# Moving GpSimd's eleven sums of x in an fp32 convolution + GELU kernel from the second product to the first

## The chip, the cores and the metric

The kernel runs on one core of one Trainium2 chip. The metric is device time in microseconds (us) of that core, the median over several executions. Four engines do the work and run independently of each other, each through its own instructions in program order: TensorE (PE in the profile) multiplies matrices, VectorE (DVE) and ScalarE (ACT) do elementwise work and read TensorE's results from PSUM, GpSimd (POOL) does elementwise work in SBUF and issues transfers of its own. SyncE (SP) only issues transfers. An engine that meets an instruction whose inputs are not there waits, and all that stands behind it on that engine waits too.

## The reference

A causal convolution of length 7 along the sequence, with one softmaxed filter for each of 8 groups of 24 channels, and behind it a two-layer block with a sigmoid-GELU, all in fp32:

```python
w = softmax(weight, axis=-1)                       # (8, 7)
x_pad = zeros(6) ++ x                              # x: (8, 4096, 192)
conv[b, s, h, :] = sum_k w[h, k] * x_pad[b, s + k, h, :]
h = conv.reshape(32768, 192) @ w_in                # (192, 2048)
g = h / (1 + exp(-1.702 * h))
out = g @ w_out                                    # (2048, 192)
```

## The kernel before

**Tiling.** The 32,768 tokens are worked through in 32 steps (`big` = 0 to 31) of 1,024 tokens. A step has two products. The *first product* makes h from the convolved x; the *second product* makes the output from g. Both are computed by bilinear schemes that save multiplications: in place of the plain block products, sums of blocks of one factor are multiplied with sums of blocks of the other, and the results are added up.

**First product.** x of a step is six blocks of 128x256 (two for each third of the 192 channels), numbered 0 to 5, and eleven sums of them, numbered 6 to 16. `SUMS_C` (line 148) lists the sums as (target, a, sign, b); block 6 is block 0 minus block 4, block 7 is block 6 minus block 5, and so on. `next_sum` (line 553) emits one, on GpSimd in all steps behind the first two. The twenty `TERMS` (line 179) pair a piece of w_in with a block of x. The product has two halves, v = 0 and v = 1, and each uses all twenty terms. `FIRST` (line 643) writes the order out by hand: "prod" is a term on TensorE (`product1`, line 588), "sum" an addition on VectorE that joins a PSUM tile and a tile in SBUF (line 636), "copy" a copy on ScalarE (line 630), "gelu" the activation that writes g (lines 612 and 617). Entries marked 1 belong to the next half and are done ahead, so the second half's terms on blocks 0, 3, 6, 7, 8, 9 and 10 run inside the first half, and seven terms of the next step open its first product. `FILL` (line 660) hangs other work in at positions of this list; `hidden` (line 757) walks both.

The six own blocks of two consecutive steps have separate places, but the eleven sums of consecutive steps share one place: the sums for step n+1 may overwrite those of step n once step n's last term on the block is through.

Each block is needed at both partition halves. `cross` (line 520) sends a group of neighbouring blocks to the other half by two transfers on SyncE's queue. Seven groups wait in a list (`pieces`): three of plain blocks, put there by `cross_blocks` (line 543), and four of sums, put there by `next_sum` when the last sum of a group is emitted. `cross_piece` (line 539) sends the list's next group.

**Second product.** g is sixteen blocks of 128x1024 (`spot(5)` to `spot(20)`); `spot(0)` to `spot(4)` are scratch of the same size. `PLAN` (line 944) is the second product's order, written out by hand. ("sum", d, a, sign, b) is an addition of two such blocks on VectorE (lines 361 and 363); ("acc", d, a) adds block a into d by a transfer that GpSimd issues (line 986); ("main", form, spot, ...) and ("side", ...) choose what TensorE multiplies next, and each ("go", n) runs n groups of four products (`go`, line 1026). "seed" is a ScalarE copy (line 1039), "join" a VectorE addition of results, "turn" a VectorE transpose, "store" the output transfer on SyncE. Between them stands work for later steps: "tap" is one of the convolution's 21 multiplications on ScalarE (line 487), "tree" adds taps by a transfer from GpSimd (line 509), "vsum" calls `next_sum`, "cross" calls `cross_piece`. After the list the loop from line 1063 does what is left of both.

**Early sums of g.** Six operations on g that need only early blocks are listed in `EARLY_G` (line 942) and hung into the first product's second half, as ("g", i): five VectorE sums and one transfer from GpSimd (block 0 into block 8).

**GpSimd's order in a step.** Twelve additions of taps (line 504) in the first product; the transfer into block 8; then in the second product the eleven sums of x mixed with six transfers of g and with the tree.

**The loop** (line 1285) emits, for each step, both halves of the first product, then puts the plain blocks of step n+1 and after them its sums on their lists, then emits the second product.

Of the kernel before, what the change touches and what calls it, by code (L numbers as in the profile page):

```python
# [15 lines left out]
def kernel(  # L16
# [49 lines left out]
    def load_x(big, ns=range(2)):  # L66


        p, c = divmod(big, CHUNKS)
        if c == 0 and 0 in ns:  # L70
            (nc.gpsimd if big else vec).memset(xin[0:R, :, 0, :], 0.0)
        for n in ns:
            for o in range(2):
                j = 1 if c == 0 and o == 0 else 0
                t = c * TOK + o * T + (j - 1) * Q
                for v in range(2):
                    q0 = o * R + v * Q
                    nc.sync.dma_start(
                        out=xin[q0 : q0 + Q, n, j:NJ, :],
                        in_=x_v[n, p, t : t + (NJ - j) * Q, v * Q : v * Q + XW].rearrange(  # L80
                            "(j i) d -> i j d", i=Q
                        ),
                    )
# [13 lines left out]
    g = consts.tile([P, NG, 2, 2, NG, T], F32)  # L97
# [341 lines left out]
    def transpose_x(big, c, n=None):  # L439
        if big not in xts:  # L440
            xts[big] = xt_pool.tile([P, NC, 2, XT], F32, name="xt")
        ns = slice(0, 2) if n is None else slice(n, n + 1)
        vec.transpose(
            xts[big][:, c, ns, :].rearrange("p n (j t) -> p (n j) t", t=Q),
            xin[:, ns, :, :].rearrange("p n j d -> p (n j) d")[:, :, c * R : c * R + Q],
        )
# [54 lines left out]
    def next_add():  # L501
        if adds:
            dst, home = adds.pop(0)
            nc.gpsimd.tensor_add(dst, dst, home)  # L504
# [10 lines left out]
    def sums_c(big, dst, a, op, b):  # L515
        add_up(
            lambda j: conv_t[:, slot_of(big, j), :], dst, a, op, b, eng=vec if big == 1 else nc.gpsimd,
        )

    def cross(big, b0, b1):  # L520
        s0, x0 = slot_of(big, b0), cross_of(big, b0)
        for o in range(2):
            nc.sync.dma_start(
                out=conv_t[halves[1 - o], x0 : x0 + b1 - b0, :], in_=conv_t[halves[o], s0 : s0 + b1 - b0, :]
            )
# [13 lines left out]
    def cross_piece():  # L539
        if pieces:  # L540
            cross(*pieces.pop(0))

    def cross_blocks(big):

        bs = list(REST)
        while bs:
            n = 1
            while n < min(3, len(bs)) and bs[n] == bs[0] + n:
                n += 1
            pieces.append((big, bs[0], bs[0] + n))  # L550
            bs = bs[n:]

    def next_sum():
        if sums_left:
            big, i = sums_left.pop(0)
            sums_c(big, *SUMS_C[i])
            for b in GROUPS:
                if max(LAST_AT[s] for s in b) == i:
                    pieces.append((big, b[0], b[-1] + 1))

    def begin_sums(big):
        sums_left.extend((big, i) for i in range(len(SUMS_C)))
# [75 lines left out]
    def plain(u, m, n, v, slot, ks=range(NC), first=0):  # L638

        for k in ks:  # L640
# [21 lines left out]
            1: (("add", 4), ("add", 4), ("add", 4)), 9: (("turn", 0),), 15: (("turn", 1),), 21: (("turn", 2),),  # L662
        },
        {
            3: (("g", 0),), 12: (("g", 1),), 17: (("g", 2),), 18: (("g", 3),), 31: (("g", 4),), 36: (("g", 5),),
        },
    ]
    FILL_1 = [
# [3 lines left out]
            32: (("work", 0.8),), 35: (("tap",),), 36: (("tap",),), 40: (("tap",),), 42: (("work", 0.8),),  # L672
        },
        {
            3: (("g", 0),), 13: (("g", 1),), 16: (("g", 2),), 17: (("g", 3),), 22: (("g", 4),), 23: (("g", 5),),
            29: (("turn", 0),), 31: (("turn", 1),), 35: (("turn", 2),),
        },
    ]

# [6 lines left out]
    def begin_half():  # L686
        return {}, dict(COUNT)
# [35 lines left out]
    def seeds_ahead(big, half):  # L723

        while later and later[0][0] == "copy":
            dst = later[0][1]
            if dst[0] == "a" and dst not in half[0] and not free:
                return
            do(big, 0, half, *later.pop(0))

    def rest_ahead(big, half):
        while later:
            do(big, 0, half, *later.pop(0))
# [6 lines left out]
    def fill(big, kind, *args):  # L740
        if kind == "work":
            work(*args)
        elif kind == "tap":
            next_tap()
        elif kind == "add":
            for _ in range(*args):
                next_add()
        elif kind == "turn":
            need(f"done {big + 1}")
            if big + 2 < N_BIG:  # L750
                transpose_x(big + 2, *args)
                if args[0] == NC - 1 and big + 3 < N_BIG:
                    load_x(big + 3)
        else:
            sum_g(*(EARLY_G if big > 1 else EARLY_G_1)[args[0]])

    def hidden(big, v, now, nxt):

        for i, (ahead, *item) in enumerate(FIRST):
            for what in (FILL if big > 1 else FILL_1)[v].get(i, ()):  # L760
                fill(big, *what)
            if not ahead:
                do(big, v, now, *item)
            elif v == 0:
                do(big, 1, nxt, *item)
            elif nxt and ahead == 2:
                do(big + 1, 0, nxt, *item)
            elif nxt:
                later.append(item)
# [162 lines left out]
    def store(big, n, o=None, queues=(nc.sync,) * 3):  # L932
# [6 lines left out]
        for c in range(NC):  # L939
            queues[c].dma_start(out=rows[c], in_=osb[c * Q : (c + 1) * Q, n, js, :])  # L940

    EARLY_G = [(6, 6, "-", 10), (1, 7, "-", 6), (1, 1, "-", 11), (0, 5, "+", 6), (8, 0, "acc"), (2, 9, "-", 0)]
    EARLY_G_1 = EARLY_G[:4] + [(8, 8, "+", 0)] + EARLY_G[5:]
    PLAN = [
        ("side", 13, 16, "k0"), ("main", 1, 5, "p2", 1), ("vsum",), ("cross",), ("go", 3), ("vsum",), ("go", 1),
# [37 lines left out]
    def sum_g(dst, a, op, b=None):  # L983

        if op == "acc":
            nc.gpsimd.dma_start(out=spot(dst), in_=spot(a), accum_op=ALU.add)  # L986
        else:
            add_up(spot, dst, a, op, b)
# [84 lines left out]
    def work(us):  # L1073
        while todo and todo[0][1] <= us + 0.2:
            us -= todo[0][1]
            todo.pop(0)[2]()

    def next_tap():
        if ready:
            ready.pop(0)[2]()  # L1080
            while ready and ready[0][1] == 0:
                ready.pop(0)[2]()

    def need(label):
        for q in (todo, ready):
            while any(item[0] == label for item in q):
                q.pop(0)[2]()
# [177 lines left out]
    def begin(big):  # L1265
        todo.extend(prepare(big))
        ready.extend(prepare_taps(big))
# [17 lines left out]
    for big in range(1, N_BIG):  # L1285
        more = big + 1 < N_BIG
        rest_ahead(big, half)
        other = begin_half()
        hidden(big, 0, half, other)
        half = begin_half() if more else None  # L1290
        hidden(big, 1, other, half)
        if more:
            need(f"done {big + 1}")
            cross_blocks(big + 1)
            begin_sums(big + 1)
        need("forms")
        if big + 2 < N_BIG:
            begin(big + 2)
        bx, bs, by = (free.pop(0) for _ in range(3))

        def final():
            free.append(bs)
            if more:
                seeds_ahead(big + 1, half)

        second(big, bx, bs, by, final, not more)
        free += [bx, by]
# [30 lines left out]
```

## Time and profile before

| what | us |
|---|---|
| median of 3 executions | 2384.64 (2384.21 to 2385.5) |
| the profiled execution, its own time | 2383.57 |
| its span, first to last instruction | 2381.9 |
| start of the first product in steps 2 and 31 | 189.1 and 2307.3 |
| first product of one step (992.99 to 1028.69) | 35.70 |
| second product of the same step (1028.69 to 1065.8) | 37.1 |
| second product of the last step (2342.80 to 2376.80) | 34.0 |
| granted TensorE clock, mean | 0.996 |

Steps 2 to 30 are 29 periods with the same work; the mean is (2307.3 - 189.1) / 29 = 73.04 us. In 22 of them the second product takes 37.1 us, in seven 37.8 to 38.3; the first product takes 35.7 to 35.9 in all.

Times in the views are counted from the first instruction. In a list of groups a line holds line of code, engine, operation, output and inputs, shapes, count, then busy us and mean ns of one, then idle time in front of them and what ended it. In a timeline a line holds start and length in us, engine, line, operation, count, and in brackets the engine's idle time before it and what released it. In a table of windows the columns are the window, its length, and for each engine its busy us with its instructions.

### The profile page before, as it was taken

The numbers are of one execution on the slowest core, as the hardware profiler recorded it, in microseconds if no ns is written. First come the engines' busy times: TensorE is split into PE (matmuls) and PEld (weight loads), VectorE is DVE, ScalarE is ACT, GpSimd is POOL, SyncE is SP. The second block draws the span as 40 slices with busy tenths as digits, with TensorE's granted clock in tenths as the row PEclk, the third lists the DMA queues.
The fourth block names the chain that finished last, engine by engine and source line by source line (L and its number), as shares of the span: only waits on it lengthen the run. The fifth ranks groups of instructions, "written<-read, shape, count | busy, mean of one in ns | idle before, by whom it ended". The sixth has DMA issues, their size and how long they took to land.

```text
span 2381.9 us, 62150 instructions
## 1 busy us (share of the span) xinstructions
PE 2285.4 (96%) x24966; PEld 1353.0 (57%) x24966; DVE 2049.1 (86%) x2842; ACT 1779.4 (75%) x3481; POOL 1133.5 (48%) x1101
## 2 busy tenths in 40 slices
PE   9899999999999999999999999999999999999999
PEld 4355555555555555555555555555555555555555
DVE  8798889988889888889888898888988889988888
ACT  8478777778777787777787777877777777778755
POOL 1454554444554446645445544556344454444520
PEclk9899999999999999999999999999999999999999
DMA  8875667655666556675556665566755567654543
GB/s 197 149 151 118 119 131 148 123 118 112 136 127 136 117 117 121 127 148 119 119 117 134 133 128 121 111 129 128 145 115 118 115 131 149 123 118 88 112 101 68
DMA packets 281073, 298.84 MB, mean 125 GB/s; under 512 B 120145, under 2 KB 212305, under 8 KB 280785
## 3 DMA queue, kind: packets, MB, share of 16 engines
q0 software_dynamic: 58080, 151.48, 35.2%
q1 hardware_dynamic: 221056, 143.00, 26.3%
q8 instruction: 197, 3.23, 0.5%
q14 instruction: 92, 0.75, 0.1%
q10 hardware_dynamic: 1648, 0.39, 0.1%
HBM read 53.15 MB, written 25.17 MB: 33 GB/s over the span
## 4 chain that ended last, share of the span: by engine, by line
PE 49%; DVE 35%; issue 7%; ACT 5%; DMA 4%; SPq 1%; POOL 0%; DVEq 0%; ACTq 0%; POOLq 0%
PE slot L595 37%; DVE g L363 16%; PE slot L1010 11%; DVE g L361 7%; DVE room L363 3%; DVE room L361 2%; DVE osbs L361 2%; ACT g L612 2%; DVE slot L636 2%; DVE room L636 1%; ACT g L617 1%; DMA conv_t<-conv_t 1%; DMA g<-osbs 1%; ACT slot L630 1%; DMA g<-g 1%
## 5 line engine op out<-in xcount | busy, mean ns | idle before, releaser
L595 PE MATMUL slot<-conv_t,w_in_s 64*128 64x512 f32 x5152 | 1154.4, 597 | 4.6 <-ACT room L630 2.3
L595 PEld LDWEIGHTS slot<-conv_t,w_in_s 64*128 64x128 f32 x5152 | 699.6, 186 | 448.4 <-issue 221.5
L1010 PE MATMUL slot<-g,w_form 128*32 128x256 f32 x9672 | 920.4, 380 | 11.4 <-DVE room L363 10.5
L1010 PEld LDWEIGHTS slot<-g,w_form 128*32 128x32 f32 x9672 | 474.1, 110 | 186.4 <-DVE room L363 25.0
L1010 PE MATMUL slot<-g,w_out_s 128*32 128x256 f32 x5952 | 470.8, 381 | 62.8 <-DVE g L363 57.6
L363 DVE TENSOR_TENSOR g<-g 128x1024 f32<-128x1024 f32 x372 | 514.2, 1408 | 8.5 <-DMA g<-osbs 3.3
L636 DVE TENSOR_TENSOR slot<-slot,room 128x512 f32<-128x512 f32 x496 | 321.9, 694 | 220.5 <-ACT g L612 118.8
L612 ACT ACTIVATE g<-slot 128x512 f32<-128x512 f32 x776 | 429.3, 610 | 75.3 <-PE slot L595 75.1
L1035 ACT COPY room<-slot 32x256 f32<-32x256 f32 x651 | 236.9, 364 | 324.8 <-PE slot L1010 233.2
L504 POOL TENSOR_TENSOR conv_t<-conv_t,g 128x512 f32<-128x512 f32 x354 | 461.9, 1308 | 23.1
L1010 PEld LDWEIGHTS slot<-g,w_out_s 128*32 128x32 f32 x5952 | 237.2, 110 | 271.3 <-issue 63.3
L630 ACT COPY room<-slot 128x512 f32<-128x512 f32 x620 | 338.5, 599 | 65.2 <-PE slot L595 43.1
L487 ACT ACTIVATE g<-xt,cw 128x512 f32<-128x512 f32 x534 | 348.9, 715 | 7.7 <-DMA g<-g 4.0
L509 POOL DMA_DIRECT2D g<-g x120 | 167.0, 1404 | 231.4 <-ACT g L487 99.9
L363 POOL TENSOR_TENSOR conv_t<-conv_t 128x256 f32<-128x256 f32 x210 | 258.8, 1297 | 2.4
L986 POOL DMA_DIRECT2D g<-osbs x30 | 26.1, 871 | 479.3 <-ACT g L612 479.3
L986 POOL DMA_DIRECT2D g<-g x124 | 115.5, 931 | 265.0 <-DVE g L363 189.6
L1010 PE MATMUL slot<-osbs,w_form 128*32 128x256 f32 x2232 | 228.8, 379 | 0.0
L361 POOL TENSOR_TENSOR conv_t<-conv_t 128x256 f32<-128x256 f32 x120 | 185.5, 1545 | 2.4
L636 DVE TENSOR_TENSOR slot<-room,slot 128x512 f32<-128x512 f32 x248 | 159.5, 689 | 27.3 <-PE slot L595 25.2
L630 ACT COPY slot<-slot 128x512 f32<-128x512 f32 x248 | 135.7, 576 | 41.1 <-PE slot L595 40.2
L636 DVE TENSOR_TENSOR room<-slot,room 128x512 f32<-128x512 f32 x248 | 159.2, 683 | 5.3 <-ACT room L630 2.1
(171 smaller groups left out, 1950.2 us busy)
## 6 DMA issues: line engine op xcount, KB each, us to landing
g<-g POOLq DMA_DIRECT2D x124, 512.0 KB, 5.5
xin<-in_x_dram SPq DMA_DIRECT2D x240, 180.0 KB, 4.1
conv_t<-conv_t SPq DMA_DIRECT2D x186, 192.0 KB, 4.3
g<-g POOLq DMA_DIRECT2D x120, 256.0 KB, 5.8
out_dram<-osbs SPq DMA_DIRECT2D x186, 128.0 KB, 3.1
conv_t<-conv_t SPq DMA_DIRECT2D x124, 128.0 KB, 3.9
g<-room POOLq DMA_DIRECT2D x31, 512.0 KB, 5.6
conv_t<-g POOLq DMA_DIRECT2D x60, 256.0 KB, 6.5
```

What stands on the lines that cost most here:

```text
L361: eng.tensor_add(v(dst), v(a), v(b))
L363: eng.tensor_sub(v(dst), v(a), v(b))
L487: act.mul(home, conv_src(big, c, k), cw[:, c, k : k + 1])
L504: nc.gpsimd.tensor_add(dst, dst, home)
L509: nc.gpsimd.dma_start(out=out, in_=src, accum_op=ALU.add)
L595: nc.tensor.matmul(slot[h], w_in_s[halves[h], a, v * P : (v + 1) * P], src, start=first, stop=True, skip_group_check=True,)
L612: act.activation(dst[:, :, h, :], src[h].rearrange("p (o t) -> p o t", o=2), AF.Gelu_apprx_sigmoid, scale=float(sign),)
L630: act.copy(bank(dst, h), bank(src, h))
L636: op(*(bank(t, h) for t in (dst, a, b)))
L986: nc.gpsimd.dma_start(out=spot(dst), in_=spot(a), accum_op=ALU.add)
L1010: nc.tensor.matmul(dst, w, t, start=first, stop=last, skip_group_check=True)
L1035: act.copy(to, d)
```

## The change

The eleven sums of x for the next step are emitted in the first product's second half instead of in the second product, for all steps but the first two. `FILL`'s second part gets "vsum" entries: five at position 0, then one each behind the terms that read the old block last. The list of sums is opened before the second half is emitted, so the four groups of sums stand ahead of the three groups of plain blocks on the list of pieces. The "vsum" entries of the second product stay, and find an empty list except in step 1.

One early sum, block 2 = block 9 minus block 0, goes from the first product's position 36 into `PLAN`; the second product's sum of block 14 goes to the head of `PLAN`. The transfer into block 8 goes from position 31 to position 20. A "tap" and an "acc" change places with a neighbour.

```diff
@@ FILL, second half
-            3: (("g", 0),), 12: (("g", 1),), 17: (("g", 2),), 18: (("g", 3),), 31: (("g", 4),), 36: (("g", 5),),
+            0: (("vsum",), ("vsum",), ("vsum",), ("vsum",), ("vsum",)), 2: (("vsum",),), 3: (("g", 0),),
+            12: (("g", 1),), 13: (("vsum",),), 17: (("g", 2), ("vsum",), ("vsum",)), 18: (("g", 3),),
+            20: (("g", 4), ("vsum",)), 26: (("vsum",),),
@@ FILL_1, second half
-            3: (("g", 0),), 13: (("g", 1),), 16: (("g", 2),), 17: (("g", 3),), 22: (("g", 4),), 23: (("g", 5),),
-            29: (("turn", 0),), 31: (("turn", 1),), 35: (("turn", 2),),
+            3: (("g", 0),), 13: (("g", 1),), 16: (("g", 2),), 17: (("g", 3),), 22: (("g", 4),), 29: (("turn", 0),),
+            31: (("turn", 1),), 35: (("turn", 2),),
@@ fill
+        elif kind == "vsum":
+            next_sum()
+        elif kind == "cross":
+            cross_piece()
@@ EARLY_G
-    EARLY_G = [(6, 6, "-", 10), (1, 7, "-", 6), (1, 1, "-", 11), (0, 5, "+", 6), (8, 0, "acc"), (2, 9, "-", 0)]
+    EARLY_G = [
+        (6, 6, "-", 10), (1, 7, "-", 6), (1, 1, "-", 11), (0, 5, "+", 6), (8, 0, "acc"),
+    ]
@@ PLAN
-        ("side", 13, 16, "k0"), ("main", 1, 5, "p2", 1), ("vsum",), ("cross",), ("go", 3), ("vsum",), ("go", 1),
-        ("sum", 14, 14, "-", 18), ("main", 16, 10, "p3", 0), ("go", 2), ("sum", 7, 8, "-", 7), ("tap",), ("go", 1),
-        ("go", 1), ("main", 0, 14, "p0", 1), ("cross",), ("go", 1), ("sum", 5, 11, "-", 19), ("go", 1),
+        ("sum", 14, 14, "-", 18), ("side", 13, 16, "k0"), ("main", 1, 5, "p2", 1), ("vsum",), ("cross",), ("go", 3),
+        ("vsum",), ("go", 1), ("main", 16, 10, "p3", 0), ("go", 1), ("sum", 2, 9, "-", 0), ("go", 1),
+        ("sum", 7, 8, "-", 7), ("tap",), ("go", 2), ("main", 0, 14, "p0", 1), ("cross",), ("go", 1),
+        ("sum", 5, 11, "-", 19), ("go", 1), ("seed", "p4", "p2", 1), ("go", 1), ("seed", "k1", "p3", 1), ("go", 1),
...
-        ("seed", "p5", "k1", 1), ("side", 19, 1, "k1"), ("acc", 14, 13), ("main", 18, 0, "p2", 0), ("go", 2),
+        ("sum", 8, 8, "-", 16), ("seed", "p5", "k1", 1), ("side", 19, 1, "k1"), ("main", 18, 0, "p2", 0),
+        ("acc", 14, 13), ("go", 2), ("vsum",), ("go", 1), ("sum", 6, 8, "-", 6), ("go", 1), ("main", 5, 8, "p1", 0),
@@ the loop over steps
         half = begin_half() if more else None
+        if more and big > 1:
+            need(f"done {big + 1}")
+            begin_sums(big + 1)
         hidden(big, 1, other, half)
         if more:
             need(f"done {big + 1}")
+            if big == 1:
+                begin_sums(big + 1)
             cross_blocks(big + 1)
-            begin_sums(big + 1)
```

More of the change, by code (lines that the diff above doesn't have):

```diff
@@ L940, in store @@
             queues[c].dma_start(out=rows[c], in_=osb[c * Q : (c + 1) * Q, n, js, :])
-    EARLY_G = [(6, 6, "-", 10), (1, 7, "-", 6), (1, 1, "-", 11), (0, 5, "+", 6), (8, 0, "acc"), (2, 9, "-", 0)]
-    EARLY_G_1 = EARLY_G[:4] + [(8, 8, "+", 0)] + EARLY_G[5:]
-    PLAN = [
-        ("side", 13, 16, "k0"), ("main", 1, 5, "p2", 1), ("vsum",), ("cross",), ("go", 3), ("vsum",), ("go", 1),
[6 rows of a table removed]
+    EARLY_G = [
+        (6, 6, "-", 10), (1, 7, "-", 6), (1, 1, "-", 11), (0, 5, "+", 6), (8, 0, "acc"),
+    ]
+    EARLY_G_1 = [
+        (6, 6, "-", 10), (1, 7, "-", 6), (1, 1, "-", 11), (0, 5, "+", 6), (8, 8, "+", 0),
+    ]
+    PLAN = [
+        ("sum", 14, 14, "-", 18), ("side", 13, 16, "k0"), ("main", 1, 5, "p2", 1), ("vsum",), ("cross",), ("go", 3),
[6 rows of a table added]
         ("sum", 0, 0, "+", 5), ("main", 14, 2, "p2", 0), ("go", 1), ("vsum",), ("go", 1), ("acc", 15, 4), ("go", 1),
```

4 rows, old and new, of the table PLAN are left out of this document.

## The prediction

> **What bounds the kernel now.** I read the page first, then the windows of one step and of the last, then TensorE's idle gaps, VectorE's groups and GpSimd's timeline around them, then ScalarE and SyncE at the step's end.
>
> ```profile
> PE 2285.4 (96%) x24966; PEld 1353.0 (57%) x24966; DVE 2049.1 (86%) x2842; ACT 1779.4 (75%) x3481; POOL 1133.5 (48%) x1101
> PE 49%; DVE 35%; issue 7%; ACT 5%; DMA 4%; SPq 1%; POOL 0%; DVEq 0%; ACTq 0%; POOLq 0%
> ```
> TensorE is the engine to beat, yet the chain that ended last runs 35% through VectorE, so TensorE is held by VectorE somewhere. The windows of a second product (step 13) and of the last step's, which prepares no next step:
> ```profile
> 1028.69:1065.83 37.14, 34.88 (x626) 20.32 (x625) 35.78 (x46) 26.76 (x57) 18.75 (x20) 1.00 0.83 164
> 2342.80:2376.80 34.00, 34.00 (x625) 20.00 (x624) 30.93 (x46) 13.06 (x34) 4.28 (x5) 1.00 0.51 98
> ```
> The same 624 products take 34.00 us there and 37.14 here; the third pair of figures is VectorE, which is busy in 35.78 of 37.14 us. TensorE's two largest gaps in step 13:
> ```profile
> 1046.40 0.42 PE L1010 MATMUL slot<-g,w_out_s 128*32 128x256 f32 x3 [1.81 <-DVE g L363]
> 1050.57 0.42 PE L1010 MATMUL slot<-g,w_form 128*32 128x256 f32 x4 [0.35 <-DVE room L363]
> ```
> Both wait for VectorE's sums of g. From start to start of a group (0.216 usual) the first costs 2.03 us in nearly every step, the second 0.72; a third, at 1058.6, 0.28. VectorE's same sums, first in step 13, then in the last step:
> ```profile
> L363 DVE TENSOR_TENSOR g<-g 128x1024 f32<-128x1024 f32 x7 | 10.0, 1480 | 0.0
> ```
> ```profile
> L363 DVE TENSOR_TENSOR g<-g 128x1024 f32<-128x1024 f32 x11 | 13.1, 1217 | 0.1
> ```
> 1480 ns against 1217 for one operation. What is beside them, GpSimd and then VectorE:
> ```profile
> 1035.00 2.76 POOL L361 TENSOR_TENSOR conv_t<-conv_t 128x256 f32<-128x256 f32 x2
> 1039.75 1.71 POOL L363 TENSOR_TENSOR conv_t<-conv_t 128x256 f32<-128x256 f32 x2
> ```
> ```profile
> 1035.53 1.64 DVE L363 TENSOR_TENSOR g<-g 128x1024 f32<-128x1024 f32 x1
> 1038.77 1.21 DVE L361 TENSOR_TENSOR osbs<-osbs,g 128x1024 f32<-128x1024 f32 x1
> 1040.23 2.31 DVE L361 TENSOR_TENSOR g<-g 128x1024 f32<-128x1024 f32 x1
> ```
> A sum of g takes 1.21 us alone, 1.64 beside one GpSimd sum of x, 2.31 behind two that follow at once. The 1.21 operation lies between two GpSimd pairs. So the eleven sums of x lengthen VectorE's list, and TensorE waits at its end.
>
> **The change, part by part.**
>
> 1. *Eleven GpSimd sums leave the second product.* Up to the first gap, VectorE loses 0.43 (1.64), 0.54 (1.75), 1.10 (2.31) and, in a pair of sums that take 3.78 together, 1.4 us: 3.5 us, more than the 2.03 of the gap. Uncontended, eleven sums at 1.14 us from start to start and a join of 0.35 end 12.9 us after VectorE's first one at 1029.74, so at 1042.6; TensorE gets to that place at 1044.4 without a gap. The gaps of 2.03, 0.72 and 0.28 go. The average second product of steps 2 to 30 takes 37.33 us (22 of 37.08, seven of 37.8 to 38.3), and 34.00 is left if nothing else holds: **-3.33 us a step**. The long seven have one VectorE sum wait 0.8 us for the transfer into block 8; its issue hangs on the same VectorE sum as before, so 7/29 of some 0.4 us stays: **+0.1**.
>
> 2. *ScalarE takes over the end.* Its last stretch in step 13:
> ```profile
> 1048.00 0.78 ACT L1035 COPY room<-slot 32x256 f32<-32x256 f32 x2 [2.99 <-DVE room L361]
> 1049.25 0.37 ACT L1035 COPY room<-slot 32x256 f32<-32x256 f32 x1 [0.47 <-PE slot L1010]
> 1049.64 3.21 ACT L487 ACTIVATE g<-xt,cw 128x512 f32<-128x512 f32 x5
> ...
> 1065.09 1.06 ACT L630 COPY slot<-slot 128x512 f32<-128x512 f32 x2
> ```
> From 1049.64 to 1065.09 it has one gap, of 0.32 us: eighteen taps and small copies, and behind them the copies that the next first product adds onto. TensorE starts that product 0.7 us after 1065.09. The stretch starts when TensorE is through the group at 1049.17, which comes 2.03 us earlier after the change, and its 0.32 goes: the copies start at 1062.74, TensorE at 1062.74 + 0.74 = 1063.5, or 34.8 us after the second product's start where TensorE alone would need 34.0. Bounds: 0 if the stretch starts earlier still, 2.0 if it does not move. It hangs on TensorE's groups in the trace, so I take **+0.85**.
>
> 3. *The sums meet VectorE in the first product's second half.* There VectorE mostly adds a PSUM tile and an SBUF tile (line 636): 0.69 us, and the same while GpSimd adds taps in the first half, so these cost nothing. Three sums of two SBUF blocks remain where GpSimd will be busy:
> ```profile
> 1020.69 1.22 DVE L363 TENSOR_TENSOR osbs<-g 128x1024 f32<-128x1024 f32 x1
> 1021.95 1.23 DVE L363 TENSOR_TENSOR osbs<-osbs,g 128x1024 f32<-128x1024 f32 x1
> 1023.71 1.30 DVE L636 TENSOR_TENSOR slot<-slot,room 128x512 f32<-128x512 f32 x2 [0.54 <-ACT g L612]
> 1024.91 1.22 DVE L361 TENSOR_TENSOR osbs<-g 128x1024 f32<-128x1024 f32 x1
> 1026.05 1.28 DVE L636 TENSOR_TENSOR room<-slot,room 128x512 f32<-128x512 f32 x2
> ```
> GpSimd's taps end at 1011.7. By TensorE's last uses of the old blocks, sum 6 starts at 1012.2, sums 7 to 9 at 1016.5, 1017.6, 1018.7 (1.03 us each, 0.08 between dependent ones), 10 and 11 at 1019.5 and 1020.3, 12 at 1022.4, 13 at 1024.3, 14 at 1025.4. Sum 11 delays the VectorE operation at 1020.69 by 0.5, which the 0.54 gap at 1023.71 takes up. Sum 13 delays the one at 1024.91 by 0.39, and this is on the path: the addition at 1026.05 feeds the GELU that the second product's first weight load waits for. Bounds: 0 if VectorE is first each time; twice 1.10 (2.31 - 1.21) less 0.54, so 1.7, if two sums are ahead each time. I take **+0.4**, by the order of starts. The skill speaks against me here: the Trainium skill, SBUF — State Buffer, section "Who interferes with whom", says of the ports that these two engines share that whoever issues first has them for the whole instruction and the other fully blocks. By that, a collision costs up to GpSimd's whole 1.03 us, the two up to 2.06 less 0.54, so 1.5, and the result would be up to 32 us poorer (1.1 more in 29 steps). The trace agrees that it is a rest of an instruction: the 1.64 is 0.43 over 1.21, beside a GpSimd sum of 1.08 us that had started 0.53 us sooner.
>
> 4. *The order of the pieces.* The sums' four groups go first, the plain blocks 0-1, 3 and 5 last. SyncE:
> ```profile
> 1065.21 5.21 SPq L940 DMA_DIRECT2D out_dram<-osbs  x6
> 1070.52 1.36 SPq L523 DMA_DIRECT2D conv_t<-conv_t  x2
> ```
> Six stores stand ahead of the seventh group, whose two transfers go out 4.7 and 5.5 us after the first product's start (1065.8). Today it is blocks 15 and 16 (128 KB, median 3.9 us to landing), used late; then it is block 5 (64 KB, median 2.1), which the tenth term multiplies, 18 groups of 0.43 us in, at 7.9. It lands at 7.6 to 9.4: a wait of 0 to 1.5. Nearest is the 64 KB row; the stores' packets ahead of it make me take **+0.3**.
>
> 5. *The rest costs nothing.* The moved sum of g already runs at 1029.74 beside the second product and only changes places with sum 14; eleven sums precede the first gap before and after, and 1.8 us of slack covers 1.14 if the order mattered. GpSimd's six transfers only lose the sums ahead of them. Without cover, one of 5 to 6 us would stop VectorE's next sum on its block.
>
> Sum: -3.33 + 0.1 + 0.85 + 0.4 + 0.3 = **-1.68 us** in each of 29 second products (steps 2 to 30; step 1 keeps its sums, the last has none): -48.7. The profiled execution, 2383.57, would be 2334.9; the median shown is 1.1 above it: **2336 us**.
>
> **The rivals.**
> - *ScalarE is no limit, and VectorE is first each time* (-3.33 + 0.1 with little else): 29 x -3.2 = -93, **2291**. For: 34.00 in the last step. Against: that step has no taps.
> - *More contention*: two collisions of 1.10, +1.7 in place of 0.4: -0.4 a step, **2373**. For: dependent sums 13 and 14 follow within 0.1 us. Against: the order of starts.
> - *Slower*: all three VectorE sums in the second half wait behind a pair at the dearest price, 1.43 (3.78 less one of 1.14 and one of 1.21): 4.3 less 0.5, +3.8 in place of 0.4: +1.7 a step, **2434**. It decides from 2.1 us lost in that half. Against: only sums 10 and 11 can follow at once; 12, 13, 14 each wait for a last use 0.9 us or more apart, or for each other.
> - *Block 5 arrives late*: at 9.4, +1.5 in place of 0.3: -0.5, **2371**; with 0.5 more of contention, no change.
> - *It does not do what it says*: a GpSimd sum held by a last use runs in the second product after all; sums 15 and 16 come at 1027.7 and 1028.5, so only a delay of many us would keep the old time, **2385**.
>
> **How the numbers follow.** Forecast 0.55, no ScalarE limit 0.12, more contention 0.14, block 5 late 0.07, no effect, from either cause, 0.04, slower 0.08. The range runs from 2298, short of the best case, to 2376, past the two weaker gains; outside are most of the best case, the slower one and no effect: 0.2. The likeliest alone: 2315 to 2350. A measurement here tells 0.2% (4.8 us) from no change; faster 0.88, same 0.04, slower 0.08.
>
> **What would show it.** VectorE's sums of g at 1.2 us throughout the second product, and no gap of TensorE at 17 us into it; else step 1 is wrong. TensorE's first weight load of the first product waiting for ScalarE, second products near 34.9: step 2. VectorE's third sum of the second half at about 1.6 and the second half some 0.4 longer: step 3. A wait of TensorE 7.9 us into the first product for a transfer: step 4. A second product still near 37 would make all of it wrong.

## The result, and the profile after

The changed kernel takes 2357.02 us (median; 2350.45 to 2361.94), the kernel before 2384.43 on the same chip: ratio 0.9884, 95% interval 0.9859 to 0.9909. It is faster by 27 us where 49 were forecast. The profiled execution is its slowest, 2361.94 us, with a span of 2360.1; the period of steps 2 to 30 falls from 73.04 to 72.34 us. From the page of the changed kernel, engines and the chain that ended last:

```profile
PE 2277.0 (96%) x24966; PEld 1351.2 (57%) x24966; DVE 1941.5 (82%) x2842; ACT 1779.5 (75%) x3481; POOL 1078.8 (46%) x1101
...
PE 66%; DVE 13%; DMA 9%; ACT 8%; issue 3%; SPq 1%; POOL 0%; DVEq 0%; POOLq 0%; ACTq 0%
PE slot L595 40%; PE slot L1020 26%; DMA g<-osbs 6%; DVE g L363 5%; ACT g L487 3%; ACT room L1045 2%; DVE g L361 1%; DVE room L363 1%; DMA conv_t<-conv_t 1%; DVE slot L636 1%; DVE osbs L361 1%; ACT slot L630 1%; DVE room L361 1%; ACT g L612 1%; DVE slot L361 1%
```

VectorE is 108 us less busy for the same 2842 instructions, and its share of the chain falls from 35% to 13%. In its place stands one transfer, g<-osbs, with 6% where it had 1%: block 0 into block 8. VectorE's largest group in the second product that starts at 1018.30 (columns as in front):

```profile
L363 DVE TENSOR_TENSOR g<-g 128x1024 f32<-128x1024 f32 x8 | 9.5, 1220 | 1.5 <-DMA g<-osbs 1.4
```

A sum of g takes 1220 ns, 1217 in the last step before the change; 1480 it was. A *group* is from here on what one ("go", 1) multiplies, eight products of the record in 0.43 us; there are 78 in a second product, counted from 0. The gaps at groups 36 and 44 (2.03 and 0.72 us) are gone. A *loss* is what TensorE needs from the start of four products to the start of the next four beyond the usual 0.216 us. But VectorE now waits, in its timeline of the same place:

```profile
1019.31 1.22 DVE L363 TENSOR_TENSOR g<-g 128x1024 f32<-128x1024 f32 x1
1020.44 1.22 DVE L363 TENSOR_TENSOR room<-g,osbs 128x1024 f32<-128x1024 f32 x1
1023.07 4.76 DVE L363 TENSOR_TENSOR g<-g 128x1024 f32<-128x1024 f32 x4 [1.41 <-DMA g<-osbs]
```

and TensorE with it:

```profile
1026.62 0.42 PE L1020 MATMUL slot<-g,w_out_s 128*32 128x256 f32 x3 [1.25 <-DVE g L363]
```

The sum of block 7 reads block 8, waits 1.41 us for the transfer, and pushes the sums behind it, of which TensorE needs one at group 16. VectorE's waits for transfers, whole run, first before the change and then after it (total us, times, longest):

```profile
DVE g L363 <- DMA g<-osbs: 3.3, 4, 1.0
```
```profile
DVE g L363 <- DMA g<-osbs: 47.5, 29, 3.1
```

The wait is there in all 29 steps. The transfer's issue has not moved: 2.0 us before the second product's start in the mean before the change, 1.9 after. It lands 5.0 us after that start in place of 3.0. What is beside it is in SyncE's and GpSimd's timelines after the change:

```profile
1016.41 6.00 SPq L523 DMA_DIRECT2D conv_t<-conv_t  x6
```
```profile
1014.79 1.59 POOL L361 TENSOR_TENSOR conv_t<-conv_t 128x256 f32<-128x256 f32 x1
1016.33 0.87 POOL L996 DMA_DIRECT2D g<-osbs  x1
1016.94 1.02 POOL L361 TENSOR_TENSOR conv_t<-conv_t 128x256 f32<-128x256 f32 x1
1017.63 1.02 POOL L363 TENSOR_TENSOR conv_t<-conv_t 128x256 f32<-128x256 f32 x1
```

Sum 14 ends at 1016.38. At 1016.41 its group, blocks 12 to 14, goes to the other partition half, 0.08 us after the transfer into block 8 was issued, and at 1018.67 the group 15-16 follows. In the table of queues from issue to landing, before and after the change, q0 is the transfer itself and q1 SyncE's (packets, MB, share of the sixteen engines' time):

```profile
q0 software_dynamic: 144, 0.52, 59.8%
q1 hardware_dynamic: 74, 0.14, 12.5%
```
```profile
q1 hardware_dynamic: 343, 0.71, 42.7%
q0 software_dynamic: 144, 0.52, 41.5%
```

0.71 MB beside the same 0.52 MB, where 0.14 were. But GpSimd's sums 15 and 16 also follow, 0.6 and 1.3 us behind the issue, and could hold up the transfer, which GpSimd issues. These are the two theories of the experiments: *transfer* (the groups of sums that leave beside it stretch it) and *sum* (GpSimd's own sums behind the issue hold it up).

### The profile page after: what moved, and what is told of

Its sections match the earlier page's. It is cut to its first block, busy times and chain, and to the rows that moved or that the text cites. A ratio compares the mean times of both kernels' runs of the same rounds, so it can differ in the third digit from the quotient of the medians.

```text
span 2360.1 us, 62266 instructions
## 1 busy us (share of the span) xinstructions
PE 2277.0 (96%) x24966; PEld 1351.2 (57%) x24966; DVE 1941.5 (82%) x2842; ACT 1779.5 (75%) x3481; POOL 1078.8 (46%) x1101
## 4 chain that ended last, share of the span: by engine, by line
PE 66%; DVE 13%; DMA 9%; ACT 8%; issue 3%; SPq 1%; POOL 0%; DVEq 0%; POOLq 0%; ACTq 0%
PE slot L595 40%; PE slot L1020 26%; DMA g<-osbs 6%; DVE g L363 5%; ACT g L487 3%; ACT room L1045 2%; DVE g L361 1%; DVE room L363 1%; DMA conv_t<-conv_t 1%; DVE slot L636 1%; DVE osbs L361 1%; ACT slot L630 1%; DVE room L361 1%; ACT g L612 1%; DVE slot L361 1%
## 5 line engine op out<-in xcount | busy, mean ns | idle before, releaser
L1020 PE MATMUL slot<-g,w_form 128*32 128x256 f32 x9672 | 900.2, 379 | 0.3 <-DVE room L363 0.3
L1020 PEld LDWEIGHTS slot<-g,w_form 128*32 128x32 f32 x9672 | 482.2, 110 | 160.2 <-DVE room L363 0.8
L363 DVE TENSOR_TENSOR g<-g 128x1024 f32<-128x1024 f32 x372 | 449.8, 1230 | 52.8 <-DMA g<-osbs 47.5
L363 POOL TENSOR_TENSOR conv_t<-conv_t 128x256 f32<-128x256 f32 x210 | 174.4, 839 | 252.6 <-PE slot L595 186.4
L509 POOL DMA_DIRECT2D g<-g x120 | 120.8, 1025 | 328.7 <-DVE room L361 118.0
L996 POOL DMA_DIRECT2D g<-g x124 | 116.2, 937 | 279.6 <-PE slot L1020 155.2
L1020 PE MATMUL slot<-osbs,w_form 128*32 128x256 f32 x2232 | 237.8, 383 | 0.2 <-ACT room L1049 0.2
L617 ACT ACTIVATE g<-room 128x1024 f32<-128x1024 f32 x124 | 132.7, 1070 | 37.9 <-DVE room L636 37.9
L1020 PEld LDWEIGHTS slot<-osbs,w_form 128*32 128x32 f32 x2232 | 117.1, 111 | 42.7 <-ACT room L1049 0.6
```

Of the source, the lines that this page charges most:

```text
L363: eng.tensor_sub(v(dst), v(a), v(b))
L509: nc.gpsimd.dma_start(out=out, in_=src, accum_op=ALU.add)
L617: act.activation(dst.rearrange("p o h t -> p h o t"), src.rearrange("p h (o t) -> p h o t", o=2), AF.Gelu_apprx_sigmoid, scale=float(sign),)
L1020: nc.tensor.matmul(dst, w, t, start=first, stop=last, skip_group_check=True)
```

## The experiments

Times are medians of four executions unless said otherwise, ratios are against the kernel before on the same chip with their 95% intervals, and "second product" is the mean of steps 2 to 30 in the profiled execution, from start to start (37.33 before, 36.47 after the change).

**Plain blocks first.** The three groups of plain blocks go ahead of the four groups of sums again; the rest of the change stays.

```diff
+            sent = pieces[:]
+            pieces.clear()
             cross_blocks(big + 1)
+            pieces.extend(sent)
```

> The changed kernel, but the three groups of plain blocks are sent to the other partition half ahead of the four groups of sums, as before the change. Transfer theory (the groups of sums 12-14 and 15-16, 384 KB and 256 KB, now leave while the transfer into block 8 is under way and stretch it from 5.0 to 6.9 us): they leave later, the transfer lands 2.7 to 3.2 us into the second product in place of 5.0, VectorE's wait for it (47.5 us in 29 steps) falls below 12, TensorE's stall of 1.7 us at group 16 goes, the second product takes 34.7 to 35.2 in place of 36.5: 2357 - 29 x 1.3 to 1.8 = 2305 to 2320. Sum theory (GpSimd's sums 15 and 16 right behind the transfer's issue hold up the writing of its descriptors): nothing changes, 2350 to 2362.

2318.86 us, ratio 0.973 (0.9715 to 0.9744). The transfer lands at 3.1, VectorE waits 2.9 us for it in the whole run (the line of its waits, as above), the mean loss at group 16 falls from 1.67 to 0.12, the second product to 35.06. The transfer theory foretold it within its ranges. The sum theory foretold no change: it falls, since sums 15 and 16 still stand where they stood.

```profile
DVE g L363 <- DMA g<-osbs: 2.9, 4, 0.8
```

**Sums 15 and 16 later.**

```diff
-            20: (("g", 4), ("vsum",)), 26: (("vsum",),),
+            20: (("g", 4),),
...
-        ("sum", 14, 14, "-", 18), ("side", 13, 16, "k0"), ("main", 1, 5, "p2", 1), ("vsum",), ("cross",), ("go", 3),
-        ("vsum",), ("go", 1), ("main", 16, 10, "p3", 0), ("go", 1), ("sum", 2, 9, "-", 0), ("go", 1),
+        ("sum", 14, 14, "-", 18), ("side", 13, 16, "k0"), ("main", 1, 5, "p2", 1), ("cross",), ("go", 3),
+        ("go", 1), ("main", 16, 10, "p3", 0), ("go", 1), ("sum", 2, 9, "-", 0), ("go", 1),
```

> The changed kernel, but sums 15 and 16 run behind GpSimd's second transfer of g, some 6 us into the second product, so that no GpSimd sum follows the transfer into block 8; the group of sums 12-14 leaves as in the changed kernel. Transfer theory: the group 12-14 still leaves with it, and the plain blocks move up to where 15-16 was; the transfer lands 4.2 to 5.0 into the second product, VectorE still waits 25 to 47 us in all; 2335 to 2362. Sum theory: the transfer lands at 2.7 to 3.2, the wait falls below 12, 2305 to 2325.

2438.54 us, ratio 1.0211 (1.017 to 1.0252): no theory's time. The landing speaks for the transfer theory all the same: 5.07 (5.03 in the changed kernel, 4.2 to 5.0 expected), with no GpSimd sum close behind the issue. The time came from elsewhere. Timelines of VectorE and GpSimd in a second product that starts at 976.0:

```profile
982.74 1.75 DVE L363 TENSOR_TENSOR g<-g 128x1024 f32<-128x1024 f32 x1
984.41 1.74 DVE L363 TENSOR_TENSOR g<-g 128x1024 f32<-128x1024 f32 x1
```
```profile
982.26 1.15 POOL L361 TENSOR_TENSOR conv_t<-conv_t 128x256 f32<-128x256 f32 x1
983.37 1.70 POOL L363 TENSOR_TENSOR conv_t<-conv_t 128x256 f32<-128x256 f32 x1
```

GpSimd's two sums meet the two sums of g that TensorE waits for at group 16, and each of those takes 0.5 us longer. TensorE's loss there grows to 3.3 us, and then this happens, in the windows (the figure behind the engines is the granted clock):

```profile
980.00:983.00 3.00, 3.00 (x60) 1.59 (x52) 1.40 (x2) 1.44 (x5) 1.30 (x2) 1.00 0.57 163
983.00:986.20 3.20, 0.10 (x4) 0.00 (x0) 3.17 (x3) 1.98 (x4) 2.07 (x2) 0.95 0.86 164
986.20:989.60 3.40, 3.39 (x36) 1.67 (x40) 3.40 (x3) 0.00 (x0) 0.76 (x1) 0.55 0.02 5
989.60:993.00 3.40, 3.40 (x72) 1.89 (x64) 3.32 (x5) 1.10 (x3) 0.97 (x2) 1.00 0.82 154
```

TensorE idles for 3.1 us, and the next 3.4 us run at half the clock: 36 products where 72 fit. The last section returns to that.

**The eleven sums alone.** `EARLY_G`, the order in `PLAN` and the transfer's position 31 are as before the change.

```diff
-            20: (("g", 4), ("vsum",)), 26: (("vsum",),),
+            20: (("vsum",),), 26: (("vsum",),), 31: (("g", 4),),
+            36: (("g", 5),),
```

> Only the eleven sums of x move; the early sum of g, the order in the second product and the transfer into block 8 (position 31, behind sums 15 and 16) are as before the change. Both theories: the transfer is issued behind two more GpSimd sums, about 0.2 us before the second product or just in it in place of 1.9 before, and lands at 5.0 to 6.5; second products 0 to 1.5 us longer than the changed kernel's 36.5, so 2357 to 2400. If the rest of the change costs and brings nothing, as predicted: 2357.

2431.35 us, ratio 1.0208 (1.0191 to 1.0226), above the range: issue at -0.01, landing at 6.13, a loss of 2.76 us at group 16, in 21 of the 29 steps with the half clock behind it. So once the sums are there, the rest of the change is worth 74 us. The trace points to the transfer's place in GpSimd's order, ahead of sums 15 and 16: without it the transfer lands 1.1 us later, and the loss is 1.1 us larger. No run moved that transfer alone.

**The rest alone.** The moved sum of g, the order in `PLAN` and position 20, with the sums of x where they were.

> The change without moving the sums of x: block 2's sum goes into the second product, sum 14 to its head, the transfer into block 8 to position 20. Prediction: VectorE runs the same sums in the same place, 2380 to 2388. If the transfer's earlier place in the program makes it leave sooner: the seven long second products shorten by 1.1 us, 2376.

2382.48 us (ten executions), ratio 0.9996 (0.9987 to 1.0006): no change, and the transfer is issued where it was. Without the moved sums the rest neither costs nor brings anything.

**The sums alone, plain blocks first.** The edits of *The eleven sums alone* and of *Plain blocks first* together.

> Only the eleven sums move, with the transfer into block 8 at position 31 behind sums 15 and 16, and the plain blocks are sent first. It separates two costs of the sums alone (2431): the transfer's late issue (0.02 us before the second product in place of 1.9) and the traffic beside it. If the issue is what counts, the transfer takes 5 us from there, lands at 5.0, and stalls TensorE by 1.6 to 2.0 us at group 16, as in the changed kernel: 2345 to 2375. If the traffic was all: landing at 2.7 to 3.2 and 2310 to 2325.

2401.3 us, ratio 1.0074 (1.0057 to 1.0091). The issue counts: landing at 5.9 with a latency of 5.9, a loss of 2.5 us at group 16 and half clock in many steps. It is worse than expected, since the plain blocks leave at the second product's start and thus beside the late transfer: landing at 5.9 and not 5.0. Of the 74 us by which the sums alone are slower than the changed kernel, the order of the pieces gives back 30.

**Only the two late groups last.** Groups 6-8 and 9-11 leave early, as in the changed kernel; 12-14 and 15-16 go behind the plain blocks.

```diff
+            late = pieces[2:]
+            del pieces[2:]
             cross_blocks(big + 1)
+            pieces.extend(late)
```

> The changed kernel, with only the groups of sums 12-14 and 15-16 put behind the plain blocks; 6-8 and 9-11 leave early, as in the changed kernel. Transfer theory, as it stands (the two groups that leave beside the transfer into block 8 stretch it): landing 2.7 to 3.2 us into the second product, 2310 to 2325 as with all four groups last. If the whole traffic ahead of it matters: landing 3.5 to 5.0, 2330 to 2357.

2307.33 us, ratio 0.9685 (0.967 to 0.9699), a little better than expected. The transfer into block 8 lands at 3.1 again, so the two groups beside it were the cause, and not the traffic ahead of it. VectorE's wait for it:

```profile
DVE g L363 <- DMA g<-osbs: 4.8, 5, 1.1
```

The kernel beats the one with all four groups last by 12 us. There the four groups leave some 4 to 10 us into the second product, beside GpSimd's next transfers: the one of block 10 into block 7 lands at 20.4 there and at 18.0 here, from the same issue at 12.3. In the whole run ScalarE's taps wait 7.4 us for such transfers there and not at all here, and the mean loss at group 62 is 0.69 there and 0.37 here; that the landing is all of the 12 us is not shown.

**Two taps earlier**, on the kernel with the plain blocks first, to test that ScalarE sets the end.

```diff
         ("go", 1), ("join", "k7", "k1", "+", "k6"), ("side", 8, 8, "k1", 2, 4), ("main", 2, 5, "p4", 0), ("vsum",),
+        ("tap",), ("tap",),
...
-        ("main", 9, 6, "p4", 0), ("vsum",), ("go", 1), ("tap",), ("tap",), ("tap",), ("go", 2),
+        ("main", 9, 6, "p4", 0), ("vsum",), ("go", 1), ("tap",), ("tap",), ("go", 2),
...
-        ("main", 21, 7, "p2", 0), ("tap",), ("tap",), ("tap",), ("go", 1), ("sum", 6, 14, "+", 6), ("go", 1),
+        ("main", 21, 7, "p2", 0), ("tap",), ("tap",), ("go", 1), ("sum", 6, 14, "+", 6), ("go", 1),
```

> The kernel with the plain blocks first (2319), and in it two of ScalarE's eighteen late taps run some 2.5 us sooner, in its idle time before group 37, the others each a place sooner. ScalarE theory (its taps and copies set the end of the second product: TensorE loses 0.69 us at group 62 and 0.27 more than before the change at the boundary): the loss at group 62 falls below 0.5, the boundary's from 0.46 to 0.2 to 0.4, the second product from 35.06 to 34.3 to 34.8, 2296 to 2312. If VectorE or TensorE itself sets the end: 2315 to 2323.

2317.01 us, ratio 0.9722 (0.9708 to 0.9737): no gain, which taken alone would speak against ScalarE. ScalarE's waits say why (first line; below it the same line of the next kernel):

```profile
ACT g L487 <- DMA g<-g: 43.9, 28, 3.5
```
```profile
ACT g L487 <- DMA g<-g: 0.3, 1, 0.3
```

The third tap overwrites block 10 and must wait until the transfer out of it has landed, at 20.5. Here the edit could tell nothing of ScalarE; it can where that transfer lands sooner, as in the next kernel.

**The same taps, with the two late groups last.**

> The kernel with the groups 12-14 and 15-16 last (2307), and in it two of ScalarE's late taps before group 37. There the transfer that reads block 10 (into block 7) lands at 17.4 to 18.5 and not at 20, so the third tap, which overwrites block 10, need not wait for it. ScalarE theory: the copies before the next first product start about 0.5 us sooner (33.97 to 33.4 in a plain step), TensorE's loss at group 62 goes from 0.37 to below 0.1, the second product from 34.77 to 34.2 to 34.4, 2291 to 2299. If ScalarE does not set the end: 2303 to 2311.

2292.89 us, ratio 0.962 (0.9606 to 0.9635), the fastest kernel that leaves nothing out. No loss is left at group 62, and a plain second product takes 34.12 us. Its window, columns as in the front:

```profile
1064.30:1098.42 34.12, 33.94 (x626) 20.05 (x625) 31.10 (x46) 26.92 (x57) 11.64 (x14) 1.00 0.86 163
```

**Two taps left out**, also on the kernel with the two late groups last.

```diff
-        act.mul(home, conv_src(big, c, k), cw[:, c, k : k + 1])
+        if big < 3 or (c, k) not in ((2, 1), (2, 2)):
+            act.mul(home, conv_src(big, c, k), cw[:, c, k : k + 1])
```

> The kernel with the groups 12-14 and 15-16 last, and two of ScalarE's eighteen late taps (the first two of the last third of the channels) left out, 1.24 us of ScalarE's last stretch; the additions that follow them stay. ScalarE theory: no loss at group 62, the second product falls from 34.77 to 34.0 to 34.2, where TensorE alone ends it, 2285 to 2293. If ScalarE does not set the end: 2303 to 2311.

2294.31 us, ratio 0.9629 (0.9613 to 0.9645), 1 us beside the expected range: plain second products of 34.10, nothing left at group 62. With 1.24 us less work ScalarE is out of the way, just as with the taps moved. So ScalarE's last stretch did set the end.

**The taps alone**, on the kernel before the change.

> The kernel before the change, with only the two late taps moved before group 37. If ScalarE sets the end only once VectorE no longer does, TensorE still waits 2.0 us for VectorE at group 36 and 0.7 at 44: 2374 to 2386. If the taps by themselves were the gain of 14 us that they brought beside the moved sums: 2365 to 2372.

2396.76 us, ratio 1.0059 (1.0043 to 1.0076): slower, which neither side expected. Before the change VectorE is late with its sum of block 20, which reads the block that the first tap overwrites; ScalarE waits, 2.6 us at most, and its copies behind wait too:

```profile
ACT g L487 <- DVE g L363: 91.6, 56, 2.6
```

The same edit costs 14 us with VectorE late and brings 14 with VectorE on time.

## Why the prediction was right, and where it was not

The direction and the mechanism were right, the size came out at little more than half. That 2357 lies inside the range is in part luck: the room above 2336 was kept for more contention and for a late block 5, and what used it was neither, but the transfer into block 8. By the prediction's parts, in us per step of the profiled executions:

1. *Sums out of the second product, -3.33 + 0.1.* The -3.33 held in its main parts: 1.90 at group 36 and 0.73 at group 44 are gone, and VectorE's sums are at 1.22. **The step that failed is the +0.1 for the transfer into block 8**, argued with "its issue hangs on the same VectorE sum as before". The issue did, and the landing did not: in place of the 0.1 the mean loss at group 16 is 1.67 (0.22 before the change), and in four of the 29 steps half clock stands behind it, about 0.2 more in the mean. Sums that end sooner send their blocks sooner, and two groups left beside the transfer on whose landing VectorE's third sum depends with no room. The prediction looked at the order of the pieces only for what comes last (part 4), and not for what now comes early. Sending the two groups later took the loss back to 0.18. That part 5 counted the rest of the change as nothing was right without the moved sums (0.9996) and wrong beside them (2431 without the rest, 2357 with it).
2. *ScalarE, +0.85.* Right in kind, a little high (34.8 less 34.0, its own figures, is 0.8): with the transfer repaired a plain second product takes 34.62 us, 0.6 over the 34.0, and 34.12 once two taps are out of the way. The copies that were forecast 34.05 us into the second product (1062.74 less 1028.69) stand at 33.97. Part of it shows at group 62, where 0.28 was forecast to go and 0.37 stayed for ScalarE's sake.
3. *Contention in the first product, +0.4.* It came as 0.1, and no end moved by it: apart from part 4's wait the first product is unchanged. Sum 13 starts ahead of VectorE's third sum of the second half, at 1013.99, but takes 0.73 us, so it is through in time, and VectorE's sum takes 1.31 us in place of 1.22 and not about 1.6:
```profile
1014.48 1.31 DVE L361 TENSOR_TENSOR osbs<-g 128x1024 f32<-128x1024 f32 x1
```
"By the order of starts" was the right way to look, but the 1.03 us for a GpSimd sum was too long: after the change only sums 15 and 16, right behind the transfer's issue, show 1.0 us, and the sums that meet nothing show 0.73. What did wait was GpSimd: sums 12 and 14 start under a sum of VectorE, and in all 29 steps each ends 0.58 to 0.59 us after that sum does (sum 14 takes 1.59 us in all). That agrees with the rule in the Trainium skill, SBUF — State Buffer, section "Who interferes with whom", that whoever issues first blocks the other. The dearer price that the prediction drew from it, a whole 1.03 us for VectorE, did not come.
4. *Block 5 late, +0.3.* It came as +0.16: TensorE waits at the tenth term of the first product for a transfer of blocks to the other half, up to 1.3 us in four steps and not at all in most. With the sums' late groups last, block 5 is no longer the last piece, and the wait is gone.
5. The sum: -1.68 forecast; -0.70 in the profiled execution, -0.94 by the medians (27.4 us in 29 steps). With the failed term repaired by the order of the pieces, which takes part 4's wait away too, it is -75 us, or -2.6 a step: more than forecast, since parts 3 and 4 then cost nothing and part 2 less.

What stays open: with the repair the transfer into block 8 still lands at 4.0 to 4.9 in three to five of 29 steps, as in four steps before the change (4.1 to 4.4). In the kernel with the two late groups last these are five steps, and in all five a 16 KB packet of the queue that the profile calls "instruction", 0.9 to 1.5 us long, runs beside the transfer. In four of the other 24 steps one does too, from 2.4 us into the second product on, and there the landing is at 2.9 to 3.3. Whether that packet is the cause no run shows.

## What to carry to other kernels

A step that is made to end sooner also sends its results sooner. For each transfer that moves, look at which other transfer is in flight then, and who waits for its landing without room. Count a collision of two engines where both will stand, and check what the freed engine meets next. The same small edit (two taps sooner) cost 14 us, brought 14 or did nothing, depending on which wait ended last.

## What the runs showed of the hardware

**Half clock behind a wait.** In the profiled executions of all twelve kernels, steps 2 to 30, a loss of TensorE at one place in the second product between 1.2 and 2.15 us was followed by half clock in 0 of 139 cases, between 2.15 and 3.0 us in 34 of 46, above 3.0 us in 36 of 37. The half clock lasts 3.41 us in 66 of these 70 cases and twice that in four; 3.41 us of it mostly cost 1.5 to 1.7. The records also show what divides the cases in between. Within one run the stretches of half clock begin whole multiples of 3.413 us apart, to 0.001 us. If the time of a run is cut into pieces at these points, each of the 70 waits with half clock has at least 2.09 us of TensorE's standstill inside one piece (counted from 0.054 us behind the start of the last product to the start of the next); of the 13 losses above 2.15 us without it, twelve have at most 2.01 us in any piece, and one has 2.22. This fits a limit of 2.1 to 2.2 us inside one piece, so that the same wait can pass or not by where it falls. The long stall of the kernel before, 2.03 us in nearly every step, lay just under it. The Trainium skill, TensorE: Matmul & The Clock Gate, section "HAM oscillation — how this bites in real kernels", gives as abstract rule that there be no idle gap of TensorE over about 3.4 us; here a loss from 2.2 us on, start to start beyond the usual 0.216, can set it off, and the measurement decides.

**Transfers of different queues slow each other.** The same 0.52 MB from GpSimd took 4.7 us beside 0.14 MB of SyncE's and 6.7 beside 0.71 (the steps of the two tables of queues). The Trainium skill, Trainium Kernel Development and Optimization, section "Key Constraints", says that transfers of all issuing engines run on the same sixteen DMA engines and interleave; the runs agree.
